# DMA transposes for two more layer norms and new weight loads in a fused attention and gated-MLP kernel

**Chip, cores, metric.** The kernel runs on one core of a Trainium2 chip. The metric is the device time of one execution in microseconds (us), compared between medians of several executions. The profiler's span of the same execution is about 1.8 us shorter than its time.

## The reference, cut to what matters

```python
def _layernorm(x, axis=-1, eps=1e-5):
    m = jnp.mean(x, axis=axis, keepdims=True)
    v = jnp.var(x, axis=axis, keepdims=True)
    return (x - m) / jnp.sqrt(v + eps)

# x: 1 x 2048 x 512 bf16; wqkv 512 x 1536, wo 512 x 512, W_gate and W_up 512 x 1376, W_down 1376 x 512
# _A_ref: 32 heads of 16; each position attends to itself and 7 earlier ones, 2 apart:
#   q.k over 8 offsets, softmax, weighted sum of v, times wo
# _B_ref: (relu(x W_gate) * (x W_up)) W_down
h  = x + _A_ref(_layernorm(x), A_wqkv, A_wo)
h2 = h + _B_ref(_layernorm(h), B_W_gate, B_W_up, B_W_down)
```

## The kernel before

The 2048 positions are worked in four chunks of 512 (chunk 0 to 3). Each chunk passes a first norm, the q, k and v projections, the attention, the output projection with the residual, a second norm and the gated MLP. A matmul needs the channels on partitions, so the normalised rows of every norm (four tiles of 128 positions) must be transposed: 8 norms, 16 transposes of 128x128 each. TensorE does it with transposes into PSUM and ScalarE evicts them; or SyncE issues four DMA transposes of 128 KB, straight into the SBUF tile `quad`.

```python
    DACC = tuple((k, t) for k in range(3) for t in range(4))      # sums done by an accumulating DMA
    DMAT = (("h",2,0),("h",2,2),("x",3,0),("x",3,2))              # norms transposed by DMA
...
                if (ln, tk, j0) in DMAT:
...
                            nc.sync.dma_start_transpose(out=dst.t[:, :, j * P:(j + 1) * P], in_=xn.t[:])
...                                                               # otherwise, on TensorE:
                            nc.tensor.transpose(tp.t[:].bitcast(BF16)[:, o:o + P],
                                                xn.t[:, t * P:(t + 1) * P], identity[:])
...                                                               # attention: v products summed over 8 offsets
                if n == 4 and (tk, t) in DACC:
                        nc.gpsimd.dma_start(mt.t[:, 0:4, :], mt.t[:, 4:8, :], accum_op=ALU.add)
```

The first halving of each sum (2 x 128x2048 elements) is not done by VectorE but by an accumulating DMA of 512 KB that GpSimd issues, four for each of the chunks 0 to 2. The order of the instructions on each engine is fixed by a table of ranks, one number for each step.

The softmax here doesn't subtract the row's maximum and nothing guards it: scores larger than these inputs give would overflow.

## Time and profile before

| | before |
|---|---|
| time, median of 3 | 203.91 us (203.57 to 204.19) |
| span of the profiled run (another execution, 205.38 us) | 203.6 us |
| TensorE busy | 195.4 us, 96% |
| VectorE busy | 155.1 us, 76% |
| ScalarE busy | 127.7 us, 63% |
| chunk 1's rows of x landed | 13.20 us |
| first matmul of chunk 0's MLP | 67.57 us |

The profile's lines are shown in the prediction. A table of slices gives the busy tenths of each engine in 40 equal slices of the span; a timeline line gives start, length, engine, source line, operation, output<-inputs, count and, in brackets, the idle time before it with what ended it. The row `PEclk` is the clock granted to TensorE, in tenths.

### The profile page before, as it was taken

To read this page: it belongs to the slowest core of one execution; us is meant where nothing else is said; L and a number is where in the kernel's file an instruction comes from. 1 tells how busy PE (TensorE), PEld (TensorE's weight loads), DVE (VectorE), ACT (ScalarE), POOL (GpSimd) and SP (SyncE) were. 2 spreads that over 40 slices of the span, in tenths; PEclk is the share of its full clock that TensorE was granted. 3 is DMA by queue.
4 is the path that set the end of the run, shared out by engine and by line. 5 is a ranking of instruction groups with operands and counts; after the bars stand their busy time and mean duration, and the time that the engine had idled before them with its cause. 6 is when DMAs were issued, how large, how long until landed. Compare 5 with 4: busy or idle time off the path is not lost.

```text
span 203.6 us, 2957 instructions
## 1 busy us (share of the span) xinstructions
PE 195.4 (96%) x1102; PEld 96.8 (48%) x1123; DVE 155.1 (76%) x246; ACT 127.7 (63%) x253; POOL 12.6 (6%) x26
## 2 busy tenths in 40 slices
PE   8499999999999999999999999999999999999994
PEld 8347545555545334444454444444444445444452
DVE  6549999999999999999999966599996255021314
ACT  3517879986569993797756599703665353576400
POOL 3000000330000002400033000000000000000000
PEclk9859999999999999999999999999999999999999
DMA  5999901698000002980059900400011001100003
GB/s 187 350 379 403 322 19 30 123 203 163 3 0 0 0 3 52 192 168 0 3 103 180 209 31 0 90 13 0 3 41 62 0 0 53 53 0 0 0 3 103
DMA packets 14893, 18.04 MB, mean 89 GB/s; under 512 B 5056, under 2 KB 12192, under 8 KB 14880
## 3 DMA queue, kind: packets, MB, share of 16 engines
q1 hardware_dynamic: 12336, 10.78, 16.4%
q0 software_dynamic: 1728, 6.29, 16.3%
q10 hardware_dynamic: 816, 0.79, 1.1%
q8 instruction: 9, 0.15, 0.3%
q14 instruction: 4, 0.03, 0.0%
HBM read 8.42 MB, written 2.10 MB: 52 GB/s over the span
## 4 chain that ended last, share of the span: by engine, by line
PE 93%; DMA 4%; issue 1%; SPq 0%; DVE 0%
PE bank L736 38%; PE bank L511 22%; PE bank L773 19%; PE bank L698 7%; DMA wq_sb<-in_A_wqkv_dram 4%; PE bank L564 4%; PE bank L465 2%; PE bank L625 1%; PE bank L597 1%; SPq L270 0%; DVE row L784 0%
## 5 line engine op out<-in xcount | busy, mean ns | idle before, releaser
L736 PE MATMUL bank<-quad,wg_sb 128*128 128x512 bf16 (+1 forms) x171 | 42.3, 379 | 0.3
L736 PE MATMUL bank<-quad,wu_sb 128*128 128x512 bf16 (+1 forms) x173 | 42.3, 379 | 0.1
L743 ACT ACTIVATE gr<-bank 128x512 bf16<-128x512 f32 (+1 forms) x44 | 26.0, 604 | 23.7 <-PE bank L736 18.3
L773 PE MATMUL bank<-wd_sb,gT 128*128 128x512 bf16 (+3 forms) x184 | 39.7, 366 | 0.2
L558 DVE TENSOR_TENSOR big<-quad,kT 128x4096 bf16<-128x4096 bf16 x16 | 36.0, 2284 | 0.1
L646 DVE TENSOR_TENSOR big<-big,vT 128x4096 bf16<-128x4096 bf16 x16 | 35.8, 2283 | 0.3 <-ACT big L631 0.3
L740 ACT CAST up_sb<-bank 128x512 bf16<-128x512 f32 (+1 forms) x44 | 25.7, 594 | 12.3 <-PE bank L736 8.5
L756 DVE TENSOR_TENSOR gT<-gr,up_sb 128x1024 bf16<-128x1024 bf16 (+1 forms) x24 | 15.4, 643 | 20.4 <-ACT gr L743 14.1
L773 PEld LDWEIGHTS <-gT 128*128 128x128 bf16 (+1 forms) x187 | 18.0, 98 | 19.3 <-issue 0.4
L736 PEld LDWEIGHTS <-wu_sb 128*128 128x128 bf16 (+1 forms) x176 | 17.3, 100 | 20.7 <-issue 1.3
L736 PEld LDWEIGHTS <-wg_sb 128*128 128x128 bf16 (+1 forms) x176 | 17.3, 100 | 20.6 <-issue 1.1
L511 PE MATMUL bank<-quad,wq_sb 128*128 128x512 bf16 (+1 forms) x70 | 16.9, 382 | 2.5 <-DMA wq_sb<-in_A_wqkv_dram 2.1
L631 ACT CAST big<-bank 128x512 bf16<-128x512 f32 x32 | 17.2, 610 | 1.5 <-PE bank L625 1.3
L511 PE MATMUL bank<-quad,wk_sb 128*128 128x512 bf16 (+1 forms) x70 | 16.8, 373 | 0.1
L678 POOL DMA_DIRECT2D big<-big x12 | 10.7, 894 | 98.3 <-DVE big L646 95.2
L784 DVE TENSOR_TENSOR row<-x_sm,bank 128x512 bf16<-128x512 bf16 (+1 forms) x17 | 10.6, 652 | 7.8 <-PE bank L773 7.8
L649 DVE TENSOR_TENSOR big<-big 128x1024 bf16<-128x1024 bf16 (+2 forms) x24 | 16.4, 727 | 0.0
L709 DVE SCALAR_TENSOR_TENSOR x_sm<-x_sm,bank 128x512 bf16<-128x512 bf16 x16 | 10.9, 685 | 6.8 <-PE bank L698 6.7
L511 PE MATMUL bank<-quad,wv_sb 128*128 128x512 bf16 x62 | 15.4, 379 | 0.1
L698 PE MATMUL bank<-wo_sb,quad 128*128 128x512 bf16 x61 | 14.8, 379 | 0.2
L371 ACT ACTIVATE row<-x_sm,mv 128x512 bf16<-128x512 bf16 x16 | 11.5, 717 | 4.5 <-DVE mv L363 4.4
L519 ACT CAST quad<-bank 128x512 bf16<-128x512 f32 x16 | 9.6, 601 | 7.4 <-PE bank L511 7.4
(65 smaller groups left out, 161.7 us busy)
## 6 DMA issues: line engine op xcount, KB each, us to landing
big<-big POOLq DMA_DIRECT2D x12, 512.0 KB, 5.5
out_dram<-row SPq DMA_DIRECT2D x15, 128.0 KB, 1.7
x_sm<-in_A_x_dram SPq DMA_DIRECT2D x3, 512.0 KB, 11.0
wu_sb<-in_B_W_up_dram SPq DMA_DIRECT2D x1, 1376.0 KB, 10.6
wg_sb<-in_B_W_gate_dram SPq DMA_DIRECT2D x1, 1376.0 KB, 13.9
wd_sb<-in_B_W_down_dram SPq DMA_DIRECT2D x1, 1280.0 KB, 15.7
wq_sb<-in_A_wqkv_dram SPq DMA_DIRECT2D x1, 512.0 KB, 8.4
wk_sb<-in_A_wqkv_dram ACTq DMA_DIRECT2D x1, 512.0 KB, 8.6
```

The lines of the kernel that those rows point to most:

```text
L371: nc.scalar.activation(out=xn.t[:], in_=h.t[:] if h else x_sm[:, tk * BPC + j, :], func=ACT.Square, bias=mv.t[:, j, 0:1], scale=1.0, accum ...
L511: nc.tensor.matmul(mm.t[:, lo:hi], lhsT=w3_sb[c][:, dt, t:D:NT], rhs=xnT.t[:, dt, lo:hi], start=(dt == 0), stop=(dt == NT - 1))
L558: V.tensor_tensor(out=pb.t[:].rearrange("p (t w) s -> p t w s", t=2), in0=q4, in1=k4, op=ALU.mult)
L631: nc.scalar.copy(out=ab.t[:, w, :], in_=bc.t[:])
L646: V.tensor_tensor(out=mt.t[:], in0=ab.t[:], in1=v8, op=ALU.mult)
L649: V.tensor_tensor(out=mt.t[:, 0:n, :], in0=mt.t[:, 0:n, :], in1=mt.t[:, n:2 * n, :], op=ALU.add)
L698: nc.tensor.matmul(od.t[:], lhsT=OT.t[:, t, j * P:(j + 1) * P], rhs=wo_sb[:, t, :], start=(t == 0), stop=(t == NT - 1 and tk not in RPE))
L736: nc.tensor.matmul(mm.t[:fs, :], lhsT=w_sb[:, dt, ft * P: ft * P + fs], rhs=hnT.t[:, dt, :], start=(dt == 0), stop=(dt == NT - 1))
L740: nc.scalar.copy(out=ub.t[:fs, i, :], in_=um.t[:fs, :])
L743: nc.scalar.activation(out=gr.t[:fs, i, :], in_=gm.t[:fs, :], func=ACT.Relu)
L756: V.tensor_tensor(out=gt.t[:fs, 0:n, :], in0=gr.t[:fs, 0:n, :], in1=ub.t[:fs, 0:n, :], op=ALU.mult)
L773: nc.tensor.matmul(od.t[:, c0:c1], lhsT=gts[ft].t[:fs, ft % 2, j * P:(j + 1) * P], rhs=wd_sb[:fs, ft, c0:c1], start=(ft == 0), stop=(ft == ...
```

## The change

The intent is to take 32 of the 96 remaining transposes off TensorE, the busiest engine, and to start it earlier. Beside the two lists below, two of chunk 0's four accumulations return to VectorE, chunk 0's second norm is split in two groups, and the rank table is new, so that every engine's order of work changes as well.

```diff
-    DACC = tuple((k, t) for k in range(3) for t in range(4))
+    DACC = tuple((k, t) for k in range(3) for t in range(4) if k or t < 2)
-    DMAT = (("h",2,0),("h",2,2),("x",3,0),("x",3,2))
+    DMAT = (('h',2,0),('h',2,2),('x',3,0),('x',3,2),('h',1,0),('h',1,2),('x',2,0),('x',2,2))
+    HG = ([[0, 1], [2, 3]], [[0, 1, 2, 3]], [[0, 1, 2, 3]], [[0, 1, 2, 3]])
...
-        for c, q in enumerate((nc.sync, nc.scalar, nc.sync)):
-            q.dma_start(w3_sb[c][:], w3_r[:, :, c * D:(c + 1) * D])
...
+        for dt, q in ((0, nc.sync), (2, nc.scalar)):
+            q.dma_start(w3_sb[0][:, dt:dt + 2, :], w3_r[:, dt:dt + 2, 0:D])
...
+        nc.gpsimd.memset(w3_sb[1][0:1, 0, 0:1], 0.0)
+        for c in (1, 2):
+            nc.sync.dma_start(w3_sb[c][:], w3_r[:, :, c * D:(c + 1) * D])
... (the other loads follow here; new RANK table, 738 numbers; faster planner loop)
```

## The prediction

> **What bounds the kernel now.** I read the page first, then the waits, TensorE's timeline, the first 26 us in half-microsecond stretches, and VectorE's timeline. The page's totals, and its table of slices:
>
> ```profile
> PE 195.4 (96%) x1102; PEld 96.8 (48%) x1123; DVE 155.1 (76%) x246; ACT 127.7 (63%) x253; POOL 12.6 (6%) x26
> ...
> PE   8499999999999999999999999999999999999994
> ...
> DVE  6549999999999999999999966599996255021314
> ```
>
> ```profile
> PEclk9859999999999999999999999999999999999999
> ```
>
> TensorE is busy to the end; the only holes and the only half-speed stretch lie before 20 us (a slice is 5.1 us). The chain of waits names the same start:
>
> ```profile
> PE 93%; DMA 4%; issue 1%; SPq 0%; DVE 0%
> ```
>
> The timeline of TensorE up to its first projections:
>
> ```profile
> 0.99 4.93 PE L489 MATMUL bank<-warm 128*128 128x128 bf16 x48 [0.99 <-DVE warm L285]
> 6.68 1.37 PE L465 MATMUL bank<-identity,row 128*128 128x128 bf16 x16 [0.76 <-DVE row L436]
> 10.13 2.32 PE L511 MATMUL bank<-quad,wq_sb 128*128 128x256 bf16 x9 [2.08 <-DMA wq_sb<-in_A_wqkv_dram]
> ```
>
> The first norm's transposes end at 8.05 us, and TensorE then stands 2.08 us for the q weights (issue 1.66 us, landing 8.4 us later). After that it runs without a wait of more than 0.3 us until 200.4 us; the tail (last output add, store, end) is 3.2 us. The matmuls from 10.13 us on are slow too: the 128x512 ones take 631 ns until about 15.6 us and 379 ns afterwards.
>
> So far this says "TensorE-bound, with a bad start". But VectorE is as tightly packed in the first half. Busy time by stretch (PE, PEld, DVE, ACT, POOL, then clock, DMA share, GB/s):
>
> ```profile
> 13.20:64.60 51.40, 50.96 (x312) 26.68 (x317) 50.43 (x80) 40.03 (x81) 3.59 (x4) 0.98 0.51 142
> 64.60:113.00 48.40, 48.08 (x296) 21.45 (x301) 48.40 (x56) 36.64 (x72) 7.14 (x8) 1.00 0.41 77
> 113.00:203.60 90.60, 87.23 (x425) 41.28 (x431) 50.07 (x87) 46.15 (x90) 0.00 (x0) 1.00 0.13 35
> ```
>
> From 13.20 to 113 us VectorE is idle for 1 us in all. The start and the end of that first stretch, with the matmul that closes it:
>
> ```profile
> 13.20 1.29 DVE L401 BATCH_NORM_STATS2 st<-x_sm 128x6 f32<-128x512 bf16 x2 [4.94 <-DMA x_sm<-in_A_x_dram]
> 63.19 1.38 DVE L436 TENSOR_SCALAR row<-x_sm,mv,rs 128x512 bf16<-128x512 bf16 x4
> 67.57 1.02 PE L736 MATMUL bank<-quad,wu_sb 128*128 128x512 bf16 x4
> ```
>
> VectorE waits 4.94 us for x of chunk 1 (landing 13.2 us), works 51.4 us until the second norm of chunk 0 leaves it (64.57 us), and 3.0 us later (transposes, eviction) the gated MLP of chunk 0 begins. By then TensorE has done nearly all q, k, v products of all four chunks: it has no other large stock of work. The two engines reach 67.57 us together.
>
> **What the Trainium skill says.** "TensorE: Matmul & The Clock Gate", Part 1: the array runs at half rate unless a free-running window of 3.4 us was busy. The trace agrees: warm-up matmuls take 311 ns until about 5.3 us and 219 ns after, and the clock is 0.5 from about 8.8 to 15.6 us, edges about one window or two apart (5.39, 8.80, 15.62 by the shares of the half-microsecond stretches). The clock column's 1.00 before 5.3 us is thus wrong; durations decide. Part 4 of the same page says that transposes do not count as busy: consistent with the fall at 8.8 us, 0.75 us after sixteen transposes, but not proved. "DMA: Bandwidth & Descriptors", "Issuing engines are not separate DMA queues": a second queue saves issue time, not bandwidth. The trace agrees: 328 to 410 GB/s from 4.5 us on, first with two queues moving and after 10 us with SyncE's alone.
>
> **The change, part by part.**
>
> *Transposes.* 32 of the 96 leave TensorE. Sixteen in a row take 1.06 us less a 0.22 us drain at 33.15 us, so 56 ns each: 32 x 56 = 1.8 us. All 64 weight loads that go were hidden. ScalarE loses four 128x1024 evictions (1036 ns each, 4.1 us), never the bound. SyncE gains eight DMA transposes of 1.2 us issue and 2.5 us landing; the norms of chunks 2 and 3 have tens of microseconds of slack. For chunk 1's second norm the new order puts about 12.2 us of products between its output projection and its MLP (8.3 us before), enough for four serial issues (4.8 us) and a landing.
>
> *Weights.* q in halves lands earlier. But in the built order the first projection on TensorE now uses the **k** weights, and k is what the GpSimd memset holds back (GpSimd's last setup step ends at 2.44 us, so k is issued near 2.7 us instead of 1.67) and sends behind q on SyncE's queue. At about 0.35 MB/us from 2.0 us, x of chunk 0, q and k (1.5 MB) are through at about 6.4 us. In this trace landings come 3 to 4 us after such averages (q at 10.1 instead of 6.1: ACT's queue has moved most of k by 7.2 us and trickles 10 packets per us until 10 us, so one or a few DMA engines lag). So k lands anywhere from 7 to 10 us; the start wins 0 to 2.0 us. The cold stretch cost (15.62 - 10.13) / 2 = 2.7 us; if TensorE starts near 8.1 to 9 us it should end one window earlier, at 12.2 us, and cost 1.6 to 2.0 us. Together TensorE alone would gain 1.8 + 1 to 3 = about 3 to 5 us.
>
> *VectorE.* Two 128x2048 additions of chunk 0 come back from GpSimd's DMA: 2 x 1.22 = 2.4 us (row of that form: 1219 ns), right inside the full stretch. Counting the new order from the first statistics of chunk 1 to the last row of chunk 0's second norm with back-to-back pitches from this trace: 12 statistics (0.63) 7.6, 12 aggregations 1.2, 12 first-norm rows (0.33) 4.0, 4 + 4 + 5 of the 128x4096 products (2.2) 28.6, two halvings of 2048 (1.15) 2.3, four of 1024 (0.60) 2.4, four last adds and four scalings (0.34) 2.7, residuals 2.6, small ones 0.6, rows 1.3: 53.3 us against 51.4 before. The split of the norm in two groups makes the rest shorter, about 2.0 us instead of 3.0 (only two rows' transposes and one eviction stand behind the last row). So the MLP of chunk 0 cannot start before T + 55.3, T being the landing of chunk 1's x; before it was T + 54.4.
>
> *The sum.* After that point the new order holds 130.4 us of warm products (512 columns at 215.8 ns and so on; the same count gives 131.9 for the kernel before, which needed 132.8), plus 0.9 of gaps, plus the tail 3.2: end = T + 55.3 + 134.5 = T + 189.8. Before: 13.2 + 54.4 + 136.0 = 203.6. With T unchanged the change is worth only 0.6 us; TensorE's 3 to 5 us are spent waiting for VectorE between 22 and 68 us. What matters is T in unprofiled runs. The profiled execution took 205.38 us for a span of 203.6, so 1.78 lies outside the span and the timed 203.91 is a span of about 202.1: T is there 11.7 us or less. Between 9.6 (2.5 MB at the average rate) and 11.7, plus up to 0.7 for the hold-back, the new span is 199.4 to 202.2, timed 201.2 to 204.0. I take 202.4.
>
> **Rivals.**
> - *TensorE is the only bound* (its table row of nines, no wait above 0.3 us). Then 203.9 - 1.8 - (1 to 3.3) = 198.8 to 201.1. Against it: VectorE's full stretch grows by 2.4 us and begins with the same load. For it: x of chunk 1 might land earlier than I think.
> - *k arrives late*, at 10 us or more, and the clock stays cold to 15.6 us again. VectorE's first product needs four projections, so it too would wait 1 to 3 us: 203.5 to 206.
> - *DMA transposes come late* (landings of 1.5 to 5.4 us in this trace, next to 512 KB accumulations) and leave TensorE idle at chunk 1's MLP: plus 0.5 to 2 us on any case. Against it: 12 us of products in between.
> - *TensorE's gain is real but a wait near 50 us is long enough to throttle the clock*: plus up to 1.7 us.
>
> **Range and chances.** Weights: VectorE-bound 0.6, TensorE-bound 0.2, late k or new waits 0.2. 2% is 4.1 us, so faster needs less than 199.8 us: part of the TensorE-bound case only. Slower needs more than 208.0, which only two bad rivals together reach. Eight times in ten: 200.2 to 204.6.
>
> **What would show it.** Right: TensorE with new waits on VectorE or ScalarE of 1 to 5 us in sum between 20 and 68 us, VectorE idle for about 1 us from the landing of chunk 1's x to the MLP of chunk 0, that MLP about 55 us after the landing, TensorE's first projection waiting for k, 32 fewer transposes. Wrong: no TensorE waits before 68 us and a span under 199 us (VectorE was not binding), or idle VectorE in that stretch (waits of its own), or TensorE waiting for a DMA transpose near 100 us.

## The result, and the profile after

| | before | after |
|---|---|---|
| time, median of 6 runs | 204.0 us (203.57 to 205.43) | 210.35 us (207.78 to 212.91) |
| ratio of the fast runs | | 1.0278, 95% interval 1.0216 to 1.0340 |
| span of the profiled run | 203.6 us | 206.0 us |
| TensorE busy | 195.4 us | 193.7 us |
| chunk 1's rows landed | 13.20 us | 11.55 us |
| first matmul of chunk 0's MLP | 67.57 us | 71.19 us |

The changed kernel is 2.8% slower. A ratio is the mean time of one kernel's fast runs over that of the other's in the same rounds, so it is not quite the ratio of the medians. One of the six runs (212.91 us) counts as slow. The profiled run is the fastest of the six; the four other fast ones take 210.2 to 210.5 us at a granted clock of 0.984 to 0.992. I come back to that with a second profile.

The page of the changed kernel, the slices of TensorE, VectorE and the clock:

```profile
span 206.0 us, 2909 instructions
...
PE   8697989499999899999999999999999999999993
...
DVE  6579999999598999999999886499984544021333
...
PEclk9999999999999999999999999999999999999999
```

The slow start is gone and the clock does not fall here. Instead TensorE has a hole in the eighth slice (36 to 41 us), and VectorE in the eleventh (51 to 57 us). The chain of waits, which was 93% TensorE, says what kind of hole it is:

```profile
PE 76%; DVE 8%; DMA 8%; ACT 4%; issue 2%; SPq 1%
```

TensorE's timeline (three lines: its first projection, the hole, the first matmuls of chunk 0's MLP):

```profile
8.57 0.63 PE L528 MATMUL bank<-quad,wk_sb 128*128 128x256 bf16 x4 [0.23 <-DMA wk_sb<-in_A_wqkv_dram]
...
39.54 1.03 PE L528 MATMUL bank<-quad,wv_sb 128*128 128x512 bf16 x4 [3.01 <-DMA quad<-row]
...
71.19 1.90 PE L753 MATMUL bank<-quad,wu_sb 128*128 128x512 bf16 x8
```

The first line answers to the 2.08 us wait at 10.13 us in the kernel before: the new loads do what they should. The second is the new loss. `quad<-row` by DMA at this place is chunk 2's first norm: TensorE has used up its other projections and stands 3.01 us until the transposes have landed. The chain around it (start, length, piece) names the last of the four transposes:

```profile
34.16 5.24 DMA quad<-row
...
39.54 14.84 PE bank L528 x68
```

That transpose was issued at 34.16 us and landed at 39.4 us. The landings of the four took 2.5, 3.9, 3.4 and 5.2 us. The DMA view of the stretch from 36 to 38 us shows what was moving meanwhile (queue, kind: packets, MB, share of the 16 engines):

```profile
q0 software_dynamic: 82, 0.34, 99.1%
q1 hardware_dynamic: 62, 0.02, 6.1%
```

Queue 0 is GpSimd's: the accumulations of chunk 0, issued at 33.6 and 36.5 us, fill the engines. Queue 1, SyncE's, which carries the transposes, gets 0.02 MB through in 2 us. From here the delay runs on. On VectorE:

```profile
11.55 1.88 DVE L418 BATCH_NORM_STATS2 st<-x_sm 128x6 f32<-128x512 bf16 x3 [3.08 <-DMA x_sm<-in_A_x_dram]
...
55.29 0.69 DVE L726 SCALAR_TENSOR_TENSOR x_sm<-x_sm,bank 128x512 bf16<-128x512 bf16 x1 [2.33 <-PE bank L715]
...
66.28 0.74 DVE L453 TENSOR_SCALAR row<-x_sm,mv,rs 128x512 bf16<-128x512 bf16 x2 [0.26 <-ACT rs L435]
```

VectorE has finished chunk 0's attention at 50.7 us, but TensorE, three microseconds late, reaches the output projection (L715) only at 54.22 us, so VectorE stands 2.33 us. The last rows of chunk 0's second norm leave it at 67.0 us, and chunk 0's MLP begins at 71.19 us.

### The profile page after: what moved, and what is told of

It reads as the page before. It is cut to its first block, busy times and chain, and to the rows that moved or that the text cites.

```text
span 206.0 us, 2909 instructions
## 1 busy us (share of the span) xinstructions
PE 193.7 (94%) x1091; PEld 94.5 (46%) x1091; DVE 156.7 (76%) x248; ACT 121.9 (59%) x251; POOL 10.6 (5%) x25
## 4 chain that ended last, share of the span: by engine, by line
PE 76%; DVE 8%; DMA 8%; ACT 4%; issue 2%; SPq 1%
PE bank L753 37%; PE bank L790 19%; PE bank L528 9%; PE bank L715 7%; DMA x_sm<-in_A_x_dram 5%; DVE big L575 3%; DVE st L418 3%; DMA quad<-row 3%; PE bank L581 2%; SPq L471 1%; DVE row L453 1%; PE bank L642 1%; ACT big L648 1%; DVE mv L421 1%; ACT ex L597 1%
## 5 line engine op out<-in xcount | busy, mean ns | idle before, releaser
L753 PE MATMUL bank<-quad,wg_sb 128*128 128x512 bf16 (+1 forms) x176 | 43.1, 379 | 0.0
L753 PE MATMUL bank<-quad,wu_sb 128*128 128x512 bf16 (+1 forms) x176 | 42.8, 379 | 0.0
L757 ACT CAST up_sb<-bank 128x512 bf16<-128x512 f32 (+1 forms) x44 | 24.7, 589 | 18.3 <-PE bank L753 17.4
L666 DVE TENSOR_TENSOR big<-big 128x1024 bf16<-128x1024 bf16 (+2 forms) x26 | 19.4, 766 | 0.1
L528 PE MATMUL bank<-quad,wv_sb 128*128 128x512 bf16 x64 | 15.9, 379 | 3.0 <-DMA quad<-row 3.0
L648 ACT CAST big<-bank 128x512 bf16<-128x512 f32 x32 | 17.1, 613 | 1.1 <-PE bank L642 0.9
L528 PE MATMUL bank<-quad,wq_sb 128*128 128x512 bf16 (+1 forms) x72 | 16.2, 356 | 0.0
L453 DVE TENSOR_SCALAR row<-x_sm,mv,rs 128x512 bf16<-128x512 bf16 x32 | 11.7, 405 | 5.0 <-ACT rs L435 4.8
L715 PE MATMUL bank<-wo_sb,quad 128*128 128x512 bf16 x64 | 15.3, 379 | 0.0
L695 POOL DMA_DIRECT2D big<-big x10 | 8.8, 877 | 102.5 <-DVE big L663 102.5
L536 ACT CAST kT<-bank 128x512 bf16<-128x512 f32 x16 | 9.3, 592 | 6.7 <-PE bank L528 5.3
```

The costliest lines, as they stand in the source:

```text
L453: V.tensor_scalar(out=xn.t[:], in0=x, scalar1=mv.t[:, j, 0:1], scalar2=rs.t[:, j:j + 1], op0=ALU.add if residual else ALU.subtract, op1=AL ...
L528: nc.tensor.matmul(mm.t[:, lo:hi], lhsT=w3_sb[c][:, dt, t:D:NT], rhs=xnT.t[:, dt, lo:hi], start=(dt == 0), stop=(dt == NT - 1))
L648: nc.scalar.copy(out=ab.t[:, w, :], in_=bc.t[:])
L666: V.tensor_tensor(out=mt.t[:, 0:n, :], in0=mt.t[:, 0:n, :], in1=mt.t[:, n:2 * n, :], op=ALU.add)
L715: nc.tensor.matmul(od.t[:], lhsT=OT.t[:, t, j * P:(j + 1) * P], rhs=wo_sb[:, t, :], start=(t == 0), stop=(t == NT - 1 and tk not in RPE))
L753: nc.tensor.matmul(mm.t[:fs, :], lhsT=w_sb[:, dt, ft * P: ft * P + fs], rhs=hnT.t[:, dt, :], start=(dt == 0), stop=(dt == NT - 1))
```

## The experiments

Four differences are mixed in the change: the loads, two additions of 128x2048 back on VectorE, two sets of DMA transposes, and the order. My theory was that chunk 2's DMA transposes cost the time because they collide with the accumulating DMAs. The rivals were that VectorE's extra work and the new order hold up the MLP, that the held-back loads cost, and that only the clock differs. Each kernel below keeps the order of all other instructions of the kernel that it is made from (d_b_h3pe alone changes the order). "Before" was measured again in each set, with a median of 203.96, 203.42 and 203.95 us in the first, second and third set. The medians in the table are over all runs; a_oldloads alone has slow ones among them (two of four).

| run | what it is | median us | ratio to before, 95% interval |
|---|---|---|---|
| a_x2pe | after, chunk 2's first norm on TensorE again | 205.89 | 1.0111 (1.0066 to 1.0155) |
| a_noacc0 | after, chunk 0's accumulations all on VectorE | 208.02 | 1.0194 (1.0152 to 1.0236) |
| a_oldloads | after, loads of before | 211.16 | 1.0242 (1.0165 to 1.0319) |
| b_loads | before, loads of after | 203.34 | 0.9965 (0.9948 to 0.9982) |
| c_after2 | after, a second profile | 210.62 | one run |
| c_b_x2 | b_loads, chunk 2's first norm by DMA | 206.45 | 1.0143 (1.0087 to 1.0198) |
| c_b_h1 | b_loads, chunk 1's second norm by DMA | 218.63 | 1.0740 (1.0688 to 1.0792) |
| c_b_acc2 | b_loads, two accumulations of chunk 0 on VectorE | 205.69 | 1.0103 (1.0054 to 1.0151) |
| d_drop0 | after, chunk 0's accumulations left out (wrong) | 206.85 | 1.0140 (1.0107 to 1.0174) |
| d_x2h1pe | after, both new sets of transposes on TensorE again | 207.04 | 1.0167 (1.0134 to 1.0201) |
| d_b_h3pe | b_loads, chunk 3's second norm earlier | 203.24 | 0.9971 (0.9953 to 0.9989) |
| d_b_h3 | the same, and that norm by DMA | 202.58 | 0.9944 (0.9927 to 0.9962) |

### a_x2pe: chunk 2's norm back on TensorE

```diff
-    DMAT = (...,('h',1,0),('h',1,2),('x',2,0),('x',2,2))
+    DMAT = (...,('h',1,0),('h',1,2))
```

> The changed kernel with one part undone: the first norm of chunk 2 is transposed on TensorE again (16 transposes, two evictions by ScalarE), so four of the sixteen DMA transposes are gone. Theory (those transposes land too late, the last at 39.4 us, and hold TensorE and all that follows up by 3 us): no wait of TensorE for rows of a DMA transpose near 36 to 40 us; the MLP of chunk 0 starts at 67 to 69 us instead of 71.2; time 203 to 206 us, so 4 to 6 us under the 210.4 us of the changed kernel, and within 1% of the kernel before. Rival (VectorE's extra additions and the new order around chunk 0's second norm hold the MLP up): its start stays at 70 us or later and the time at 208 us or more. Rival (only the clock differs from run to run): profile and timed runs keep the 2.5 us between them.

The wait is gone and the time falls to 205.89 us; the ratio falls from 1.0278 to 1.0111, so this part alone costs about 1.7%, or 3.4 us. The theory holds for the larger half of the loss. The MLP of chunk 0, however, starts at 69.53 us, not at 67 to 69 us, so something of the rival is true too. Its line in TensorE's timeline shows one thing more:

```profile
69.53 3.48 PE L753 MATMUL bank<-quad,wu_sb 128*128 128x512 bf16 x8
```

Eight matmuls take 3.48 us here and 1.90 us in the changed kernel's profile: in this profiled run TensorE ran at half speed for 3.4 us from 69.3 us on. The three timed runs have clocks of 0.997 to 1.000, so it is not the rule, but the profile of d_drop0 shows the same at the same place.

### a_noacc0 and d_drop0: the collision taken away

In the first, VectorE does the two additions that GpSimd's DMAs did. In the second, nobody does them, so that VectorE's work stays equal; its result is wrong.

```diff
# a_noacc0
-    DACC = tuple((k, t) for k in range(3) for t in range(4) if k or t < 2)
+    DACC = tuple((k, t) for k in range(1, 3) for t in range(4))
# d_drop0
                 if n == 4 and (tk, t) in DACC:
+                    if tk == 0:
+                        continue
```

> The changed kernel without GpSimd's two accumulating DMAs in chunk 0 (issued at 33.6 and 36.5 us); VectorE does their additions, about 2.4 us more on its way to chunk 0's attention. Theory (the 512 KB of the accumulation keep the engines busy while chunk 2's transposes want to land): the third and fourth transposes of chunk 2 land in under 3 us after issue instead of 3.4 and 5.2, and TensorE's wait for them falls from 3.0 us to under 1.5; the MLP of chunk 0 comes at about the same 71 us, because VectorE's 2.4 us lie on that path; time 207 to 211 us. Rival (the transposes are late because they are issued late, one after the other, and the accumulation does not matter): the landing times stay at 3.4 and 5.2 us and the wait at 3 us, and the time goes up to 211 to 213 us.

> The changed kernel without GpSimd's two accumulating DMAs in chunk 0, and without anything in their place: chunk 0's result is wrong on purpose, and all else is as in the changed kernel. It takes the collision away and adds no work to VectorE. Theory (the collision with these 2 x 512 KB is the whole cause of the late landing): every DMA transpose of chunk 2 lands in about 2.5 us, TensorE waits less than 0.5 us for them, no stretch at half speed follows, time 204.5 to 206.5 us against 210.4 of the changed kernel. Rival (the transposes are issued too late anyway, one after the other): a wait of 2 us or more stays and the time is above 208 us.

The DMA view (output<-input, queue, operation, count, median us from issue to landing) of the first norms of chunks 2 and 3, first in the changed kernel (26 to 50 us), then in d_drop0 (28 to 50 us; a_noacc0 gives the same 2.5), with TensorE's wait for chunk 2 in d_drop0:

```profile
quad<-row SPq DMA_TRANSPOSE x8, 3.6
```

```profile
quad<-row SPq DMA_TRANSPOSE x8, 2.5
```

```profile
37.30 1.03 PE L528 MATMUL bank<-quad,wv_sb 128*128 128x512 bf16 x4 [0.36 <-DMA quad<-row]
```

Without the accumulations the median landing is 2.5 us. Of chunk 2's own four, however, only the last one changes: 2.5, 4.0, 3.6 and 2.5 us in d_drop0 against 2.5, 3.9, 3.4 and 5.2 us in the changed kernel (4.6, 3.7, 3.2 and 2.5 us in a_noacc0). So it is not the accumulations that slow the second and third, though I had expected it; what does is not shown. The fourth is the one that TensorE waits for: its wait for chunk 2 shrinks from 3.01 us to 0.36 us in d_drop0 and to nothing above 0.2 us in a_noacc0 (where a wait of 1.05 us for chunk 3's transposes comes instead, at 45.78 us). So the collision is the cause of the wait in the change's order; the rival "issued too late anyway" is refuted there, though the issues alone use up all the time that there is. The times are 206.85 us (a little over the range that I gave) and 208.02 us: a_noacc0 pays two more additions (2.4 us) and is 1.2 us slower in medians, with both ratios good to about 0.4%. In d_drop0 the DMA transposes of chunk 2 still bring no gain over a_x2pe (1.0140 against 1.0111, intervals overlapping), as is to be expected where VectorE sets the length (c_b_acc2 below). Two of its four runs have a clock of 0.991, the profiled one among them. That profile shows where: TensorE is at half speed from 68.7 to 72.1 us, at the start of chunk 0's MLP, with no wait above 0.4 us listed in the 30 us before. What sets it off there is open.

### a_oldloads and b_loads: the loads alone

```diff
# a_oldloads: the loads of before in the changed kernel; b_loads: the reverse
-        for c, q in enumerate((nc.sync, nc.scalar, nc.sync)):
-            q.dma_start(w3_sb[c][:], w3_r[:, :, c * D:(c + 1) * D])
+        for dt, q in ((0, nc.sync), (2, nc.scalar)):
+            q.dma_start(w3_sb[0][:, dt:dt + 2, :], w3_r[:, dt:dt + 2, 0:D])
+        # ... k, v, x and the rest after nc.gpsimd.memset(w3_sb[1][0:1, 0, 0:1], 0.0)
```

> The changed kernel with the loads of the kernel before (q weights whole on one queue, k on the other, nothing held back by GpSimd). Theory (the loads are the good part of the change): TensorE starts its projections at about 10 us instead of 8.6, chunk 1's rows land near 13 us instead of 11.6, the wait for chunk 2's transposes stays within 2 to 4 us; time 210 to 213 us, 0 to 2.5 us above the changed kernel. Rival (the held-back loads are what costs): time 205 to 208 us.

> The kernel before with nothing but the new loads (q weights in halves on both queues, others held back). Theory (loads are a gain of 1 to 2 us, for chunk 1's rows come 1.6 us earlier and TensorE starts 1.5 us earlier at a warm clock): MLP of chunk 0 at 66 to 67 us instead of 67.6; time 201.5 to 203.5 us against 204. Rival (the held-back loads are what costs): 206 us or more.

b_loads settles it: 203.34 us, ratio 0.9965, a gain of 0.35% whose interval leaves out 1. It is thus a version that beats both kernels. The gain is at the low end of my range, probably because the cold start of the kernel before is not in most of its runs: the profiled one has a clock of 0.983, but in 10 of the 14 runs in that set it is 1.000. a_oldloads has two fast runs of four (207.56 and 210.16 us), and its interval covers the changed kernel's ratio, so it says nothing on the loads' size; its profile shows the same wait for chunk 2 (3.24 us).

### c_after2: where a slower run of the changed kernel loses 2.8 us more

> The changed kernel itself, for one more profile: the first one is its fastest run (span 206.0 us, clock 0.998), its other fast runs have spans of 208.4 to 208.7 us at a clock of 0.984 to 0.992. Theory (the wait for chunk 2's DMA transposes is longer there and then costs a stretch at half speed): TensorE waits 3 to 4.5 us for rows of a DMA transpose near 36 to 40 us, the matmuls after it take about twice 216 ns for one to three us, span 208 to 209 us. Rival (the clock falls elsewhere, such as in the thin stretch of transposes and small matmuls before the MLP of chunk 0): the slow matmuls are near 65 to 72 us and the wait is 3 us as before.

The kernel is unchanged; the second profile (span 208.8 us, clock 0.984) has the length of the four other fast runs. TensorE's timeline:

```profile
39.50 1.87 PE L528 MATMUL bank<-quad,wv_sb 128*128 128x512 bf16 x4 [3.19 <-DMA quad<-row]
41.16 1.91 PE L528 MATMUL bank<-quad,wk_sb 128*128 128x512 bf16 x4
42.87 1.91 PE L528 MATMUL bank<-quad,wq_sb 128*128 128x512 bf16 x4
44.57 1.43 PE L528 MATMUL bank<-quad,wk_sb 128*128 128x512 bf16 x4
45.84 1.03 PE L528 MATMUL bank<-quad,wq_sb 128*128 128x512 bf16 x4
```

The wait is 3.19 us instead of 3.01, and the four groups after it are slow: 1.87, 1.91, 1.91 and 1.43 us instead of 1.03 us each. By the starts, 39.50 to 45.84 us for four groups that took 39.54 to 43.00 us in the first profile, that is 2.9 us lost, and the spans differ by 2.8 us. By the clock column TensorE is at half speed from 38.6 us, still inside the wait, to 45.4 us. This is what the Trainium skill warns of in "TensorE: Matmul & The Clock Gate", section "Why this matters for your kernels", which advises against idle gaps over about 3 us between bursts. The runs agree only in part. The clock fell around the waits of 3.19 us here and 3.24 us in a_oldloads, and held through 3.01 us in the first profile; but it also fell after a wait of only 2.33 us (c_b_x2, below), and at chunk 0's MLP in a_x2pe and d_drop0 with no such wait near. So these runs give no edge in the length of a wait. In these four runs the half speed lasted 3.4 us each time, and here twice that, 6.8 us.

My theory's numbers hold for this run; the rival's place near the MLP does not show in it. One run does not speak for all: of the four other fast runs one has this clock of 0.984, and three have 0.990 to 0.992, which is about half to two thirds of the time at half speed, and yet they take as long. What else they lose is not shown.

### c_b_x2 and c_b_h1: each set of DMA transposes alone, in the old order

```diff
-    DMAT = (("h",2,0),("h",2,2),("x",3,0),("x",3,2))
+    DMAT = (("h",2,0),("h",2,2),("x",3,0),("x",3,2),("x",2,0),("x",2,2))   # c_b_x2
+    DMAT = (("h",2,0),("h",2,2),("x",3,0),("x",3,2),("h",1,0),("h",1,2))   # c_b_h1
```

> The kernel before with the new loads and with chunk 2's first norm by DMA transposes, every other instruction in its old order. Theory (those transposes land late, next to the accumulation): TensorE, which wants chunk 2 at about 30 us there, waits 4 to 7 us for it, with a stretch at half speed after it; time 208 to 212 us against 203.3 for the same kernel with these transposes on TensorE. Rival (it is the new order of the other instructions that costs, and the engine has enough other products): within 1 us of 203.3.

> The kernel before with the new loads and with chunk 1's second norm by DMA transposes, every other instruction in its old order. Theory (these transposes are the good part: TensorE saves 1.06 us and has products to do meanwhile): no wait of over 0.5 us for rows near 100 us; time 202 to 203 us, 0.5 to 1.1 us under the 203.3 us with the new loads alone. Rival (8 us of products are too few for four issues of 1.25 us and a landing): a wait of 1 us or more there and 203.5 to 205 us.

c_b_x2 costs 1.8% against b_loads (1.0143 against 0.9965), nearly the same as in the change's order, but the mean is below the 208 us that I expected. TensorE waits 2.33 us for chunk 2, and its clock falls 1.2 us after the wait. The two landings in the chain took 2.40 and 2.47 us, so nothing collided here. The loss has another path, which VectorE's timeline shows:

```profile
30.18 1.69 DVE L451 TENSOR_SCALAR row<-x_sm,mv,rs 128x512 bf16<-128x512 bf16 x5
33.40 0.41 DVE L451 TENSOR_SCALAR row<-x_sm,mv,rs 128x512 bf16<-128x512 bf16 x1 [1.52 <-DMA quad<-row]
34.80 0.41 DVE L451 TENSOR_SCALAR row<-x_sm,mv,rs 128x512 bf16<-128x512 bf16 x1 [0.99 <-DMA quad<-row]
36.20 0.41 DVE L451 TENSOR_SCALAR row<-x_sm,mv,rs 128x512 bf16<-128x512 bf16 x1 [0.98 <-DMA quad<-row]
36.53 8.89 DVE L661 TENSOR_TENSOR big<-big,vT 128x4096 bf16<-128x4096 bf16 x4
```

The program has five buffers for `row`, and in this order VectorE writes the eight rows of chunks 2 and 3 one after the other. From the sixth on it stands until a DMA transpose has landed and given its buffer back, 3.5 us in all. The eight rows take 6.4 us; in b_loads they take 2.6 us (28.64 to 31.21 us). Then VectorE works without a wait above 0.2 us until the MLP of chunk 0, which starts 56.5 us after the landing of chunk 1's rows (11.98 to 68.48 us) instead of 53.4 us. These 3.1 us match the loss in the medians (206.45 against 203.34 us). A run with more row buffers, which would test this, was not made. In the changed kernel's order the rows are spread, and VectorE has no wait for a row buffer.

c_b_h1 was the surprise. I expected a gain and it is 7.4% slower than before. The chain and TensorE's timeline, where chunk 1's MLP begins:

```profile
105.52 10.94 DMA quad<-row
```

```profile
116.59 3.53 PE L751 MATMUL bank<-quad,wg_sb 128*128 128x512 bf16 x8 [13.78 <-DMA quad<-row]
```

The same DMA transpose that lands in 2.5 us alone took 10.94 us. In the old order GpSimd issues the four accumulations of chunk 2 at 99.8, 103.3, 105.5 and 107.9 us, and SyncE the transposes from 99.9 us on. TensorE stands 13.78 us and then runs at half speed (eight matmuls in 3.53 us). The change's order had put chunk 1's transposes before those accumulations (issued from 100.7 to 106.7 us; the accumulations follow at 106.3, 108.7, 110.7 and 112.9 us, and TensorE has no wait there), so there they did no harm. No run takes the accumulations away from c_b_h1, so that they are the cause here is read from the trace and from d_drop0, not shown by an experiment of its own.

### d_x2h1pe: what chunk 1's set is worth where nothing collides

```diff
-    DMAT = (...,('h',1,0),('h',1,2),('x',2,0),('x',2,2))
+    DMAT = (("h",2,0),("h",2,2),("x",3,0),("x",3,2))
```

> The changed kernel with both new sets of DMA transposes undone: chunk 2's first norm and chunk 1's second norm are transposed on TensorE again; against the run that undid chunk 2 alone (205.9 us) it tells what chunk 1's set is worth. Theory (TensorE is the bound there, with products in stock): its 1.06 us of transposes come back in full, 206.5 to 207.2 us. Rival (VectorE is full until 113 us, so TensorE's saving is lost): 205.6 to 206.2 us.

207.04 us against 205.89 us for a_x2pe, a difference of 1.15 us in medians (1.0167 against 1.0111). The intervals overlap, and the two ran in different sets, so this is not clear of noise. The value is near that of the 16 transposes (1.06 us with the drain of the last; by the starts in a_x2pe, 34.07 to 34.96 us, they hold TensorE for 0.89 us), so chunk 1's set is most likely a gain in the change's order.

### c_b_acc2: two additions back on VectorE, in the old order

```diff
-    DACC = tuple((k, t) for k in range(3) for t in range(4))
+    DACC = tuple((k, t) for k in range(3) for t in range(4) if k or t in (0, 3))
```

> The kernel before with the new loads and with two of chunk 0's four accumulations back on VectorE as two additions of 128x2048 (2.4 us), every other instruction in its old order. Theory of the prediction (VectorE is full until the MLP of chunk 0 begins, so what it gets is paid in full): TensorE gets waits of 1.5 to 2.5 us for VectorE before 68 us, and the time is 204.5 to 206 us against 203.3. Rival (TensorE has enough other products then): no new wait, 203 to 203.8 us.

The ratio goes from 0.9965 to 1.0103, 1.4% or 2.8 us (good to about 1 us) for 2.4 us of work: paid in full. (The change itself puts back the other pair, t = 2 and 3.) The stretch from the landing of chunk 1's rows to chunk 0's MLP (length, then busy time and count of TensorE, its weight loads, VectorE, ScalarE and GpSimd, then clock, DMA share, GB/s), for b_loads and for c_b_acc2:

```profile
10.44:63.84 53.40, 52.80 (x351) 27.78 (x350) 53.03 (x81) 42.32 (x85) 3.59 (x4) 1.00 0.55 153
```

```profile
11.37:66.64 55.27, 52.59 (x346) 27.38 (x345) 55.10 (x83) 41.84 (x84) 1.88 (x2) 1.00 0.42 126
```

VectorE is busy for 53.03 of 53.40 us and for 55.10 of 55.27 us. The stretch grows by 1.87 us and VectorE's work in it by 2.07 us, while TensorE's does not grow. VectorE sets the length of this stretch.

### d_b_h3 and its control: a norm with nothing beside it

If collisions and short stock are the reasons, a norm without them should gain. Chunk 3's second norm qualifies: the last accumulation is issued at 107.9 us. I put its output projection's groups together, which makes the rows ready 3.8 us earlier (from 157.85 us in d_b_h3, from 161.63 us in b_loads; d_b_h3pe is the control with this order), and then gave the transposes to the DMA (d_b_h3).

```diff
-    DMAT = (("h",2,0),("h",2,2),("x",3,0),("x",3,2))
+    DMAT = (("h",2,0),("h",2,2),("x",3,0),("x",3,2),("h",3,0),("h",3,2))
# both runs, order on TensorE: wo3 wo0 wo2 wo1 of chunk 3 in a row; VectorE: its residual adds and rows before gu4 gu5
```

> The kernel before with the new loads and, near 150 us, the four groups of chunk 3's output projection one after the other instead of spread, so that chunk 3's second norm is ready earlier; its transposes stay on TensorE. The control for the next run. All theories: 203.0 to 203.7 us, the same as with the new loads alone.

> The same with chunk 3's second norm by DMA transposes. Theory (a DMA transpose is worth its 16 x 66 ns where no accumulation is under way and some 10 us of products lie between the rows and their use, and in the last 90 us nothing but TensorE is full): landings of 2.5 us, no wait for them, time 1.06 us under the control, 202.0 to 202.7 us. Rival (the output stores on the same queue, or four issues one after the other, make them late): a wait of 1 us or more near 166 us and no gain.

```profile
158.33 5.13 SPq L469 DMA_TRANSPOSE quad<-row  x4
```

```profile
163.96 4.50 PE L788 MATMUL bank<-wd_sb,gT 128*128 128x512 bf16 x20
168.29 1.03 PE L751 MATMUL bank<-quad,wu_sb 128*128 128x512 bf16 x4
```

SyncE issues the four between 158.33 and 163.46 us, they land in 2.5 us (median), and TensorE passes from its other products to the MLP at 168.29 us with no wait in brackets. The time is 202.58 us against 203.24 us for the control in the same rounds, 0.66 us less (intervals of 0.9927 to 0.9962 and 0.9953 to 0.9989, which just overlap; the means of the 9 and 22 runs are 202.66 and 203.33 us). That is less than the full 1.06 us, and nearer to the 0.91 us that the 16 transposes take in the control by the starts; at 0.6% under the kernel before it is the best version.

## Why the prediction was wrong

The prediction said 202.4 us with a range of 200.2 to 204.6, and that only two bad rivals together would make it slower by over 2%. It is 210.35 us. Of the signs of being wrong that it named, idle VectorE in the full stretch came (3.0 us); a wait for a DMA transpose near 100 us did not. Step by step:

- **The loads** were right. The first projection waits for k (0.23 us), at 8.57 us, 1.56 us earlier and inside the 0 to 2.0 us; chunk 1's rows land at 11.55 us, inside the 9.6 to 11.7 us plus hold-back. Their worth in timed runs is 0.35% (b_loads).
- **VectorE's bill** was right as a bill. From the landing at 11.55 us to the last row at 67.0 us pass 55.5 us, of which VectorE works 52.4 us, against the 53.3 us counted, and stands 3.0 us. That VectorE is what binds this stretch is shown by c_b_acc2.
- **The step that failed** is in the part on transposes: "the norms of chunks 2 and 3 have tens of microseconds of slack". The first of chunk 2's transposes is issued at 29.3 us and TensorE wants the last at 36.5 us: 7.2 us. The fourth is issued 4.9 us after the first and lands 2.5 us later when alone, so there was no slack at all, and 5.2 us later next to an accumulation. I had the row "landings of 1.5 to 5.4 us … next to 512 KB accumulations" in front of me and placed it, as a rival, at chunk 1's MLP, where the new order had avoided it. (The 1.5 us in that row belongs to output stores from the same buffers; the DMA transposes took 2.4 to 5.4 us.) That the collision makes the wait is shown by d_drop0; the wait makes VectorE stand 2.33 us at the output projection.
- **A second step was mis-sized**: "about 2.0 us instead of 3.0" from the last row to the MLP. It is 4.2 us (67.0 to 71.19), and 4.2 us as well without any DMA transposes of chunk 2 and chunk 1 (in d_x2h1pe, 65.2 to 69.33 us). ScalarE's timeline in the changed kernel shows what I had not looked at, three evictions of chunk 1's attention weights (L648) between the two halves of the norm's transposes (L496), and the MLP starts only after the second half. In TensorE's own order chunk 1's attention products (L642, L581) also stand before the MLP, and the chain runs through them; no run separates the two:

```profile
67.67 1.03 ACT L496 COPY quad<-bank 128x1024 bf16<-128x1024 bf16 x1
68.57 1.58 ACT L648 CAST big<-bank 128x512 bf16<-128x512 f32 x3
70.00 1.07 ACT L496 COPY quad<-bank 128x1024 bf16<-128x1024 bf16 x1
```

  Together: 55.3 + 3.0 - 0.9 + 2.2 = 59.6, measured 71.19 - 11.55 = 59.6 us after the landing.
- **After the MLP's start** the count held: 206.0 - 71.19 = 134.8 us against 134.5.
- **The clock** was a rival with "plus up to 1.7 us" for a wait near 50 us. It came at 38.6 us, and cost 2.9 us in the one run that was profiled with it (c_after2). The steps above account for the first profile (207.78 us); the 2.6 us from there to the median are explained only as far as that run goes.
- **Smaller slips** that did not decide: 32 weight loads go with the 32 transposes, not 64; one half-microsecond stretch after 4.5 us (8.0 to 8.5 us) shows only 246 GB/s; and the 1.5 us between the profiled and the timed runs of the kernel before were put down to an earlier landing T, while those runs differ in clock (0.983 against 1.000 in most), so that reading is not shown.

Over the ratios, the loss adds up as a ladder of runs. Each step is the difference of two ratios, so good to 0.5 to 0.8%, or 1 to 1.6 us, but for the first:

| step | from, to | ratio | change |
|---|---|---|---|
| new loads | before, b_loads | 0.9965 | -0.35% |
| two additions on VectorE | b_loads, c_b_acc2 | 1.0103 | +1.4% |
| order, split norm | c_b_acc2, d_x2h1pe | 1.0167 | +0.6% |
| chunk 1's second norm by DMA | d_x2h1pe, a_x2pe | 1.0111 | -0.6% |
| chunk 2's first norm by DMA | a_x2pe, after | 1.0278 | +1.7% |

So the two steps of 0.6% are not clear of noise, and the row "order, split norm" is a remainder. The 4.2 us behind the last row belong to it, but it also shortens the rest after the MLP's start (135.7 us in d_x2h1pe against 136.6 us in c_b_acc2). I did not take it apart further.

## What to carry to other kernels

A DMA transpose is not a free transpose: it is a transfer with a deadline. Before moving one, write down when its rows leave, when the consumer has run out of other work, which large transfers are issued in between, and how many row buffers the transposes hold until they land. The gain was 0.7 us (d_b_h3) and perhaps 1.1 us (d_x2h1pe) for 16 transposes, and none where VectorE set the length (d_drop0); the loss was 3 to 15 us where an accumulation or the row buffers got in the way. Where TensorE waits 2 us or more in mid-kernel, reckon with a stretch at half speed around it: such a stretch slowed TensorE by 1.7 us in c_b_x2 and by 2.9 us in c_after2.

## What the Trainium skill lacked or had wrong

- "Advanced Engine Details and Errata", section "X-Bar Transpose (TRN2)", says that transpose DMAs are as fast as regular ones. Here a 128 KB transpose takes 2.5 us from issue to landing when alone, and a 128 KB output store 1.7 to 1.8 us; the store goes to HBM, and no run has a plain copy inside SBUF of this size, so the comparison is not like for like. Each transpose also holds SyncE for about 1.3 us (5.13 us for four in d_b_h3), and for 2.2 us on average with the queue busy (8.71 us for four in c_b_h1); no page gives a time for trn2 of issuing a transpose of this size.
- "DMA: Bandwidth & Descriptors", section "Issuing engines are not separate DMA queues", says rightly that all issuers share the same engines, but not what that does to latency. Next to GpSimd's accumulations of 512 KB the landing rises from 2.5 us to 5.2 us (two of them, d_drop0 against the changed kernel) and to 10.9 us (among four of them, in c_b_h1).
